# Fused cosine attention and gated product on one core: loads, turns and stores on one queue, V cast on chip, the last pair of each batch turned by TensorE

## The chip, the core and the metric

The kernel runs on one core of a Trainium2 chip. The core has five engines with queues of their own: TensorE (PE, with its weight loads shown as PEld), VectorE (DVE), ScalarE (ACT), GpSimd (POOL) and SyncE (SP). Each runs its instructions in the order in which they were written into its queue, and waits on semaphores for the others. DMA transfers are issued here from SP and from POOL. The metric is the device time of one execution in microseconds.

## The reference

Eight batches, twelve heads, 448 positions of 64 numbers. Rows of q and k are brought to length one, scores are divided by tau = 0.1, softmax and the product with v follow. The result, with heads side by side as 768 columns, goes through two weight products with `h * cos(h)` between them.

```python
q_n = q / (np.linalg.norm(q, axis=-1, keepdims=True) + 1e-06)
k_n = k / (np.linalg.norm(k, axis=-1, keepdims=True) + 1e-06)
scores = np.matmul(q_n, k_n.transpose(0, 1, 3, 2)) / tau
attn = np.exp(scores - np.max(scores, axis=-1, keepdims=True))
attn = attn / (np.sum(attn, axis=-1, keepdims=True) + 1e-09)
x = np.matmul(attn, v).transpose(0, 2, 1, 3).reshape(B * S, H * D)
h = x @ w_in                      # 768 to 2048
return (h * np.cos(h)) @ w_out    # 2048 to 768
```

## The kernel before

**Tiles.** A *pair* is two heads; three pairs are a *unit* (half a batch), six pairs a batch; there are 48 pairs and 16 units. The 448 positions lie as 4 x 112, so most tiles have 112 partitions.

**Work of a unit.** `load` brings k and q as fp32 into `raw` (two buffers, so unit u+2 can be loaded only when unit u has been scaled). `square` makes `sq` (mostly on POOL, line 683), `reduce` sums it on DVE (line 690), `rnorm` makes 1/length on ACT by a logarithm and an exponential (lines 698 and 701), `scale` writes the normed rows to `qks` in bf16 (POOL, line 709). `load_v` brings V through POOL's queue into `vin`, cast to bf16 by the DMA, and `copy_v` copies it to `va`, beside a column of ones (DVE for units 0 to 3, POOL later, line 659).

**Work of a pair.** `transposes` turns `qks` into `qkT`: the first nine pairs by PE and a DVE copy (lines 732, 740), the others by a DMA transpose on SP (line 724). `scores` multiplies on PE into the PSUM tiles SC0 and SC1 (line 749) and ACT takes the exponential into `PX` (line 754). `attend` multiplies with `va` into the PSUM tile AV (line 771), DVE divides by the sums into `xs` (lines 780, 781), and `xs` is turned into `xT`: by a DMA transpose on SP (line 787), except for pairs 4 and 5, which PE turns into the PSUM bank PO (line 795) with a DVE copy behind it (line 799).

**Work of a batch.** `m1` is the first weight product: eight groups of twelve products into SC0, SC1 or AV (line 812), a cosine on ACT (line 826, the sine table with a quarter turn), a product on DVE into `gT` (line 828). It reads all six `xT` of its batch and stands behind the first pair of the next batch. ACT loads another table before and after it (line 606). The second product (M2, line 862) runs by tiles of 128 rows in two halves, 16 products each, into PO or PO2; DVE copies each half to one of three buffers `osb` (line 869), and SP stores the tile (line 873). M2 fills PE's gaps between scores.

**Order.** All operations are written down as a list with reads and writes. `arrange` then plays the list through a table of costs and picks for every engine the next operation that is ready and due first; an operation with a large negative `bias` counts as due early. `emit` writes the queues, computes the waits, and puts idle products on zeros (`zt`, line 897) into long planned gaps of PE. So a changed cost, bias or dependency can move work on all engines. The parts that matter most here:

```python
XPE = (4, 5)
o = P.op(eng, ..., cost=(0.75 if eng == "POOL" else 0.46) * len(fns),
         dma=sem, bulk=bulk, label=label, bias=-100.0 if eng == "POOL" else 0.0)
if p == 0 and 2 <= u < NU - 1:
    load(4, 0, UP, eng="POOL") if u == 2 else None
    copy_v(u + 1)
    load_v(u + 2) if u < NU - 2 else None
if 3 <= u < NU - 2:
    load(u + 2, p, p + 1)
```

Units 2, 3 and 4 and all of V go through POOL's queue, as do the weights W1 and W2 in four parts each (lines 886 and 892); units 0, 1 and those from 5 on go through SP, pair by pair.

Of the kernel before, what the change touches and what calls it, by code (L numbers as in the profile page):

```python
# [482 lines left out]
def bass_cosine_attention__then__act_gcu_kernel(  # L483
# [10 lines left out]
    DM = NH * D  # L494
# [57 lines left out]
    zt = sb("zt", [128, S], BF16)  # L552
    iot = sb("iot", [NP, NP], I32)
# [30 lines left out]
    MM = S / 2400.0 + 0.0025  # L584
    MH = HW / 2400.0 + 0.0025

    def dma(eng, fns, reads, writes, sem, bulk=0.0, label="", behind=None, pkt=0.013):
        o = P.op(eng, lambda e: [f(e) for f in fns], reads, writes, cost=(0.75 if eng == "POOL" else 0.46) * len(fns),
                 dma=sem, bulk=bulk, label=label, bias=-100.0 if eng == "POOL" else 0.0)
        o.nd, o.pkt = len(fns), pkt  # L590
        if behind is not None:
            P.order_only(behind, o)
        return o
# [54 lines left out]
            if eng == "POOL":  # L648
                pooled[0] = P.ops[-1]

    def load_v(u):
        i = u % 2
        dma("POOL", [lambda e: e.dma_start(vin[i].ap().rearrange("p (h c) -> p h c", h=UH), src(v, u, 0, UH))],
            (), [("vin", i)], "vin%d" % i, 2.3, "load v u%d" % u, pooled[0], 0.055)
        pooled[0] = P.ops[-1]

    def copy_v(u):
        i = u % 2
        f = lambda e: e.tensor_copy(vav[i][:, :, 0:D], vinv[i])  # L659
# [103 lines left out]
    def attend(g):  # L763
        u, p, j, y = g // UP, g % UP, g % 2, g % NX
        i, b, n = u % 2, g // PB, D + 1

        def av(e, a):
            for x in range(NJ):
                k = a * S + NP * x
                for c in range(NJ):  # L770
                    t = e.matmul(AVv[:, a, n * x : n * x + n], PXv[j][:, c, k : k + 128],  # L771
                                 vav[i][:, NJ * (2 * p + a) + c, 0:n], start=(c == 0), stop=(c == NJ - 1))
            return t

        P.group = len(P.ops)
        for a in range(2):
            P.op("PE", lambda e, a=a: av(e, a), [("va", i)] + [("PX", j, c) for c in range(NJ)], ["AV"],
                 cost=NJ * NJ * 0.0304, mode="F", label="AV%d" % g)
        P.group = None
        dve(lambda e: e.reciprocal(rcpv[y], AXv[:, :, :, D]), ["AV"], [("rcp", y)], 8 * NS, label="rcp%d" % g)  # L780
        dve(lambda e: e.tensor_tensor(  # L781
            xsv[y].rearrange("p x h d -> p h x d"), AXv[:, :, :, 0:D],
            bass.AP(rcp[y], 0, [[NS, NP], [NJ, 2], [1, NJ], [0, D]]), ALU.mult),
            ["AV", ("rcp", y)], [("xs", y)], NS * D, label="xs%d" % g)
        to = ("xT", b % 2, g % PB)
        if g not in XPE:
            dma("SP", [lambda e: e.dma_start_transpose(
                xTv[b % 2][:, g % PB, :].rearrange("p (x m) -> p x m", x=NJ), xs[y].ap())],
                [("xs", y)], [to], "xT%d" % y, 0.4, "X%d" % g, None, 0.014)
            P.ops[-1].cost = 0.8  # L790
            return

        def turn(e):
            for x in range(NJ):
                r = e.transpose(XTv[:, NP * x : NP * x + NP], xsv[y][:, x, :, :], ident.ap())
# [56 lines left out]
    def m2_emit(n=10 ** 6):  # L852
        for t, hf in m2_queue[:n]:
# [14 lines left out]
            o = t % 3  # L868
            dve(lambda e, po=po, o=o, hf=hf: e.tensor_copy(osb[o].ap()[:, HW * hf : HW * hf + HW], po[:, 0:HW]),  # L869
                keys, [("osb", o, hf)], HW, label="osb%d" % t)  # L870
            if hf == 1:
# [12 lines left out]
    def load_w1(x):  # L884
        w = FF // NQ
        pooled[0] = dma("POOL", [lambda e: e.dma_start(
            W1v[:, :, w * x : w * x + w], bass.AP(moe_w_in.tensor, w * x, [[FF, 128], [128 * FF, NKC], [1, w]]))],
            (), [("W1", x)], "W1_%d" % x, 4.2, "W1.%d" % x, pooled[0], 0.09)

    def load_w2(x):  # L890
        w = NF // NQ
        pooled[0] = dma("POOL", [lambda e: e.dma_start(
            W2v[:, w * x : w * x + w, :], moe_w_out[128 * w * x : 128 * w * (x + 1), :].rearrange("(f p) n -> p f n", p=128))],
            (), [("W2", x)], "W2_%d" % x, 4.2, "W2.%d" % x, pooled[0], 0.13)

    zero = dve(lambda e: e.memset(zt.ap(), 0.0), (), ["zt"], S)  # L896
    P.filler = {n: (lambda e, t=t: e.matmul(t.ap()[:, 0:S], zt.ap()[:, 0:128], zt.ap(), start=True, stop=True))  # L897
                for n, t in (("PO", PO), (("TP", 0), PO2))}, zero, MM, 0.3
# [3 lines left out]
    pairs = [P.ops[-PB + x] for x in range(PB)]  # L902

    def find(label):
        return [o for o in P.ops if o.label == label][-1]
# [43 lines left out]
    norms(0, 0)  # L949
    transposes(0)  # L950
    norms(0, 1)
    load_v(0)
    after(P.ops[-1], pairs[1])
    load_w1(0)
    after(P.ops[-1], pairs[3])
    load_v(1)
    load_w1(1)
    copy_v(0)
    copy_v(1)
    for g in range(PB):  # L960
        pair(g)
    load(2, 0, UP, eng="POOL")
    load_w1(2)
    load_w1(3)
    load_v(2)
    load_w2(0)
    load_w2(1)
    norms(2, 0)
    load(3, 0, UP, eng="POOL")
    load_w2(2)  # L970
    load_w2(3)
    load_v(3)
    for g in range(PB, BYPE):
        transposes(g)
    attend(PB - 1)
# [17 lines left out]
    banks[0] = banks[0] + [(n, x[:, 0, :]) for n, x in PHs]  # L993
    m2_emit()
    P.arrange()
    P.emit(nc, ["out%d" % o for o in range(3)])
    ctx.close()
    return P

# [32 lines left out]
```

## Time and profile before

| | us |
|---|---|
| median of 3 runs | 481.06 |
| lowest and highest run | 480.97, 484.44 |
| the profiled execution, its time | 482.17 |
| its span, first to last instruction | 480.4 |
| PE busy | 444.1 |
| of that, idle products on zeros | 29.2 |
| ACT, DVE, POOL busy | 264.0, 212.8, 209.3 |

The profile shows one execution. A row of a timeline gives the start and the length in us, the engine, the line in the kernel, the operation, the tile written and the tile read, the shapes, how many instructions were merged, and in brackets how long the engine sat idle before and what released it. "SPq" is SP's queue at work on issuing a transfer; the transfer itself lands later. PE is busy for 92% of the span, so what matters is where the other 36 us and the idle products lie, and what stands at the end of those waits. The name of a releaser is that of the instruction which came last; where that instruction had itself been waiting, the cause is one step further back.

### The profile page before, as it was taken

Reading aid. Unit: us, or ns where it says so; the run is one execution under the profiler, and the core shown is the slowest. Engines: PE = TensorE matmul, PEld = TensorE weight load, DVE = VectorE, ACT = ScalarE, POOL = GpSimd, SP = SyncE. Lnnn points to the kernel's source line nnn. Section 1 sums busy time; section 2 is a strip of 40 time slices with the busy share of each in tenths; the row PEclk is TensorE's granted clock in tenths of the full one; section 3 lists DMA queues with packets and bytes.
Section 4 is the critical chain, followed back from the end, with each engine's and each line's share of the span. In section 5 each row is a group of like instructions: output and inputs, shape, how many; then the busy total and the mean of one; then the engine's idle time right before and its main releaser. Section 6 shows DMA issues by size and latency. Waiting matters only on the chain.

```text
span 480.4 us, 8869 instructions
## 1 busy us (share of the span) xinstructions
PE 444.1 (92%) x3787; PEld 236.5 (49%) x3787; DVE 212.8 (44%) x286; ACT 264.0 (55%) x319; POOL 209.3 (44%) x140
## 2 busy tenths in 40 slices
PE   8997999998999499996999949999799999999996
PEld 4453545544555255553555515555445545555563
DVE  5555575537534344353533534435643344225311
ACT  4855368883588125881477604786258756844100
POOL 3988528978088410894029540296408300000000
PEclk9998899999999889997999979999999999999999
DMA  8999998999089910899009990199504700320122
GB/s 220 183 193 202 226 229 102 237 223 246 0 98 216 215 33 0 170 203 222 2 11 163 170 217 0 44 205 210 137 0 107 125 11 1 78 71 0 34 81 84
DMA packets 98919, 59.63 MB, mean 124 GB/s; under 512 B 60896, under 2 KB 94240, under 8 KB 98880
## 3 DMA queue, kind: packets, MB, share of 16 engines
q1 hardware_dynamic: 81472, 43.14, 42.6%
q0 software_dynamic: 17408, 15.93, 22.4%
q8 instruction: 30, 0.49, 0.4%
q14 instruction: 9, 0.07, 0.1%
HBM read 45.61 MB, written 11.01 MB: 118 GB/s over the span
## 4 chain that ended last, share of the span: by engine, by line
PE 56%; POOL 20%; ACT 9%; issue 6%; DMA 5%; DVE 2%; SPq 1%; POOLq 0%; ACTq 0%
PE SC L812 20%; PE AV L812 12%; PE PO L862 11%; POOL qks L709 9%; POOL sq L683 6%; ACT PX L754 5%; PE AV L771 4%; DMA xT<-xs 4%; PE PO L897 3%; PE SC L749 3%; POOL va L659 3%; PE SC L862 2%; ACT L606 2%; DMA raw<-in_q_dram 2%; ACT cosb L826 1%
## 5 line engine op out<-in xcount | busy, mean ns | idle before, releaser
L754 ACT ACTIVATE PX<-SC 112x896 bf16<-112x896 f32 x192 | 164.8, 914 | 30.9 <-PE SC L749 30.8
L862 PE MATMUL PO<-W,gT 128*128 128x384 bf16 x816 | 151.2, 330 | 13.6 <-DVE osb L869 13.6
L709 POOL TENSOR_TENSOR qks<-raw,rn 112x1024 bf16<-112x1024 f32 x47 | 88.6, 1909 | 119.5 <-ACT rn L701 119.4
L812 PE MATMUL SC<-xT,W 128*128 128x448 bf16 x480 | 101.1, 367 | 11.7 <-DMA xT<-xs 9.0
L862 PEld LDWEIGHTS PO<-W,gT 128*128 128x128 bf16 x816 | 73.6, 98 | 74.3 <-issue 19.2
L826 ACT ACTIVATE cosb<-SC,cst 128x896 f32<-128x896 f32 x40 | 40.2, 1007 | 105.0 <-PE SC L812 104.9
L683 POOL TENSOR_TENSOR sq<-raw 112x1024 bf16<-112x1024 f32 x42 | 79.2, 1907 | 34.6 <-DMA raw<-in_q_dram 34.4
L690 DVE TENSOR_REDUCE n<-sq 112x16 f32<-112x1024 bf16 (+1 forms) x49 | 58.3, 1193 | 53.5 <-POOL sq L683 49.0
L812 PEld LDWEIGHTS SC<-xT,W 128*128 128x128 bf16 x480 | 48.0, 101 | 59.8 <-issue 21.0
L828 DVE TENSOR_TENSOR gT<-SC,cosb 128x896 bf16<-128x896 f32 x40 | 43.6, 1091 | 45.7 <-ACT cosb L826 45.4
L749 PE MATMUL SC<-qkT 64*128 64x448 bf16 x384 | 58.2, 357 | 3.7 <-ACT PX L754 0.9
L812 PE MATMUL AV<-xT,W 128*128 128x448 bf16 x288 | 58.5, 352 | 0.7
L771 PE MATMUL AV<-va,PX 112*128 112x65 bf16 x1536 | 57.1, 193 | 0.5 <-ACT PX L754 0.5
L771 PEld LDWEIGHTS AV<-va,PX 112*128 112x128 bf16 x1536 | 51.5, 97 | 10.9 <-issue 8.9
L869 DVE COPY osb<-PO 128x384 f32<-128x384 f32 x51 | 28.2, 553 | 40.8 <-PE PO L862 40.8
L780 DVE RECIPROCAL rcp<-AV 112x8 f32<-112x8 f32 x48 | 9.9, 206 | 74.0 <-PE AV L771 74.0
L812 PEld LDWEIGHTS AV<-xT,W 128*128 128x128 bf16 x288 | 27.7, 98 | 28.6 <-issue 3.1
L826 ACT ACTIVATE cosb<-AV,cst 128x896 f32<-128x896 f32 x24 | 24.2, 1007 | 30.9 <-PE AV L812 30.8
L828 DVE TENSOR_TENSOR gT<-AV,cosb 128x896 bf16<-128x896 f32 x24 | 26.2, 1091 | 25.7 <-ACT cosb L826 25.5
L749 PEld LDWEIGHTS SC<-qkT 64*128 64x128 bf16 x384 | 14.6, 93 | 42.7 <-ACT PX L754 25.9
L781 DVE TENSOR_TENSOR xs<-AV,rcp 112x512 bf16<-112x512 f32 x48 | 33.2, 691 | 2.0
L897 PE MATMUL PO<-zt 128*128 128x448 bf16 x123 | 29.2, 379 | 1.6 <-DVE zt L896 1.6
(37 smaller groups left out, 144.4 us busy)
## 6 DMA issues: line engine op xcount, KB each, us to landing
raw<-in_k_dram SPq DMA_DIRECT2D x39, 224.0 KB, 5.4
raw<-in_q_dram SPq DMA_DIRECT2D x39, 224.0 KB, 6.1
vin<-in_v_dram POOLq DMA_DIRECT2D x16, 336.0 KB, 7.6
W<-in_moe_w_in_dram POOLq DMA_DIRECT2D x4, 768.0 KB, 17.8
W<-in_moe_w_out_dram POOLq DMA_DIRECT2D x4, 768.0 KB, 29.1
out_dram<-osb SPq DMA_DIRECT2D x8, 336.0 KB, 3.6
out_dram<-osb SPq DMA_DIRECT2D x8, 288.0 KB, 2.6
raw<-in_k_dram POOLq DMA_DIRECT2D x3, 672.0 KB, 18.9
```

The source lines that it names most:

```text
L683: pool(lambda e, x=x, y=y: e.tensor_tensor(y, x, x, ALU.mult), src_, dst, 0.1 + n * 1.78e-3, label="sq%d.%d" % (u, p))
L690: dve(lambda e, w=w: e.tensor_reduce(out=n2v[i][:, 2 * p : 2 * p + 2, w], in_=sqv[p][:, :, w, :], axis=mybir.AxisListType.X, op=ALU.add), ...
L709: f = lambda e, s0=s0, s1=s1: e.tensor_tensor(qksv[i][:, p, s0:s1, :, :].rearrange("p s h d -> p h s d"), rawv[i][:, h, s0:s1, :], bass.AP ...
L749: t = e.matmul(SCv[z][:, a, 0:S], qkT[k].ap()[r, NP * c : NP * c + 128], qkT[k].ap()[r, S : 2 * S], start=True, stop=True)
L754: act(lambda e: e.activation(PXv[j][:, c, 0 : 2 * S].rearrange("p (a s) -> p a s", a=2), SCv[z][0:NP, :, 0:S], ACT.Exp, scale=1.0 / TAU), ...
L771: t = e.matmul(AVv[:, a, n * x : n * x + n], PXv[j][:, c, k : k + 128], vav[i][:, NJ * (2 * p + a) + c, 0:n], start=(c == 0), stop=(c == N ...
L781: dve(lambda e: e.tensor_tensor(xsv[y].rearrange("p x h d -> p h x d"), AXv[:, :, :, 0:D], bass.AP(rcp[y], 0, [[NS, NP], [NJ, 2], [1, NJ], ...
L812: t = e.matmul(ph[:, a, 0:S], W1v[:, c, 128 * n : 128 * n + 128], xTv[b % 2][:, c, :], start=(c == 0), stop=(c == NKC - 1))
L826: act(lambda e, ph=ph, cz=cz: e.activation(cosv[cz], ph[:, :, 0:S], ACT.Sin, bias=cst.ap()[:, 0:1], scale=1.0), names(gi) + ["cst0"], [("c ...
L828: dve(lambda e, ph=ph, cz=cz, gi=gi: e.tensor_tensor(gTv[:, 2 * gi : 2 * gi + 2, S * (b % 2) : S * (b % 2) + S], ph[:, :, 0:S], cosv[cz], ...
L862: r = e.matmul(po[:, 0:HW], gTv[:, y, col : col + 128], W2v[:, y, HW * hf : HW * hf + HW], start=(y == 0), stop=(y == NF - 1))
L897: P.filler = {n: (lambda e, t=t: e.matmul(t.ap()[:, 0:S], zt.ap()[:, 0:128], zt.ap(), start=True, stop=True)) for n, t in (("PO", PO), ((" ...
```

## The change

It has six parts, and new costs that go with them.

1. Pairs that PE turns: all of batch 0 and the last pair of every batch (11, 17 ... 47) instead of pairs 4 and 5 only. The turn now goes into AV instead of PO.
2. All loads of q, k and V are issued from SP. Units from 2 on are loaded whole (two transfers of 672 KB instead of six of 224 KB).
3. V stays fp32 in `vin`. `copy_v` casts it, on DVE for units 0 and 1 and on POOL from unit 2 on.
4. V of units 0 and 1 stands between the first loads on SP; the weights wait for V of unit 0, and all but the first two parts of W1 have a small bias (-10) instead of -100, so that unit 2 comes ahead of them in the plan.
5. Four buffers for stores instead of three.
6. The planner's costs of DMA issues, turns, AV products and the V copy are changed.

```diff
-    XPE = (4, 5)
+    XPE = set(range(PB)) | set(range(PB - 1, NG, PB))
+    NO = 4
+    WB = -10.0
-    vin = sbs("vin", 2, [NP, UH * NJ * D], BF16)
+    vin = sbs("vin", 2, [NP, UH * NJ * D], F32)
-    osb = sbs("osb", 3, [128, DM], F32)
+    osb = sbs("osb", NO, [128, DM], F32)
-    XTv = PO.ap().bitcast(BF16)
+    XTv = AV.ap().bitcast(BF16)
...
-        o = P.op(eng, ..., cost=(0.75 if eng == "POOL" else 0.46) * len(fns),
-                 dma=sem, bulk=bulk, label=label, bias=-100.0 if eng == "POOL" else 0.0)
+        o = P.op(eng, ..., cost=(0.8 if eng == "POOL" else 0.52) * len(fns),
+                 dma=sem, bulk=bulk, label=label, bias=bias)
...
-    def load_v(u):
+    def load_v(u, eng="SP"):
...
-        if u < 4:
-            dve(f, [("vin", i)], [("va", i)], UH * NJ * D / 2, lock=True, label="va%d" % u)
+        if u < 2:
+            dve(f, [("vin", i)], [("va", i)], UH * NJ * D, label="va%d" % u)
         else:
-            pool(f, [("vin", i)], [("va", i)], 0.1 + UH * NJ * D * 1.2e-3, label="va%d" % u)
+            pool(f, [("vin", i)], [("va", i)], 1.46, label="va%d" % u)
...
-                [("xs", y)], [to], "xT%d" % y, 0.4, "X%d" % g, None, 0.014)
-            P.ops[-1].cost = 0.8
+                [("xs", y)], [to], "xT%d" % y, 0.7, "X%d" % g, None, 0.014)
+            P.ops[-1].cost = 1.25
...
-        P.op("PE", turn, [("xs", y), "ident"], ["PO"], cost=NJ * 0.0487, mode="F", label="XP%d" % g)
-        dve(lambda e: e.tensor_copy(xTv[b % 2][:, g % PB, :], XTv[:, 0:S]), ["PO"], [to], S, label="xT%d" % g)
+        P.op("PE", turn, [("xs", y), "ident"], ["AV"], cost=NJ * 0.0487, mode="F", label="XP%d" % g)
+        dve(lambda e: e.tensor_copy(xTv[b % 2][:, g % PB, :], XTv[:, 0:S]), ["AV"], [to], S / 2, label="xT%d" % g)
...
     for g in range(PB):
-        load(g // UP, g % UP, g % UP + 1, g == 0, "SP", P.ops[-1] if g else None)
+        load(g // UP, g % UP, g % UP + 1, g == 0)
+        if g % UP == UP - 1:
+            load_v(g // UP)
...
-            load(4, 0, UP, eng="POOL") if u == 2 else None
             copy_v(u + 1)
-            load_v(u + 2) if u < NU - 2 else None
-        if 3 <= u < NU - 2:
-            load(u + 2, p, p + 1)
+            if u == 2:
+                load(4, 0, UP)
+                load_v(4)
+        if 3 <= u < NU - 2 and p == 1:
+            load(u + 2, 0, UP)
+            load_v(u + 2)
...
-    load_v(0)
-    after(P.ops[-1], pairs[1])
     load_w1(0)
-    after(P.ops[-1], pairs[3])
-    load_v(1)
+    after(P.ops[-1], find("load v u0"))
     load_w1(1)
...
-    load(2, 0, UP, eng="POOL")
+    load(2, 0, UP)
```

How the plan moved is seen at three places. The first is SP's queue before batch 3's first product: `xT1<-xs4` and `xT1<-xs5` are the turns of that batch's fifth and sixth pair, `qkT` are turns of later pairs, `raw1` are loads two units ahead. Before:

```order
L787 DMA_TRANSPOSE xT1<-xs4 128x4x112
L724 DMA_TRANSPOSE qkT4<-qks1 128x8x112
L724 DMA_TRANSPOSE qkT5<-qks1 128x8x112
L640 DMA raw1<-in_k_dram 112x2x256
L640 DMA raw1<-in_q_dram 112x2x256
L640 DMA raw1<-in_k_dram 112x2x256
L640 DMA raw1<-in_q_dram 112x2x256
L787 DMA_TRANSPOSE xT1<-xs5 128x4x112
```

After:

```order
L727 DMA_TRANSPOSE qkT4<-qks1 128x8x112
L642 DMA raw1<-in_k_dram 112x6x256
L642 DMA raw1<-in_q_dram 112x6x256
L790 DMA_TRANSPOSE xT1<-xs4 128x4x112
L727 DMA_TRANSPOSE qkT5<-qks1 128x8x112
L876 DMA out_0_dram<-osb2 16x768
L876 DMA out_0_dram<-osb2 112x768
L655 DMA vin1<-in_v_dram 112x6x256
```

The sixth pair's turn is gone from the queue; the fifth pair's now stands behind a whole unit's k and q, and a load of V has come in.

The second is POOL's queue at the start, from the second scale of unit 0 (`qks0`) to the first squares of unit 1 (`sq<-raw1`). Before:

```order
L709 TENSOR_TENSOR qks0<-raw0,rn0 112x2x8x64
L640 DMA raw0<-in_k_dram 112x6x256
L640 DMA raw0<-in_q_dram 112x6x256
L886 DMA W1<-in_moe_w_in_dram 128x6x512 x2
L653 DMA vin0<-in_v_dram 112x6x256
L892 DMA W2<-in_moe_w_out_dram 128x4x768 x2
L683 TENSOR_TENSOR sq0<-raw1 112x1024
```

After:

```order
L889 DMA W1<-in_moe_w_in_dram 128x6x512 x2
L712 TENSOR_TENSOR qks0<-raw0,rn0 112x2x8x64
L686 TENSOR_TENSOR sq0<-raw1 112x1024
L889 DMA W1<-in_moe_w_in_dram 128x6x512 x2
L686 TENSOR_TENSOR sq1<-raw1 112x1024
```

The loads of unit 2 and of V have left POOL, and the other weights have moved behind unit 1's first squares.

The third is DVE's queue ahead of batch 2's first product: `n20` and `n21` are the sums of squares of the next two units, `osb` the copies out of PO and PO2, `gT` the first products of M1. Before:

```order
L869 COPY osb2<-PO 128x384
L690 TENSOR_REDUCE n20<-sq2 112x16
L690 TENSOR_REDUCE n21<-sq0 112x16
L869 COPY osb2<-PO2 128x384
L690 TENSOR_REDUCE n21<-sq2 112x16
L869 COPY osb0<-PO 128x384
L690 TENSOR_REDUCE n21<-sq1 112x16
L828 TENSOR_TENSOR gT<-SC0,cosb0 128x2x448
```

After:

```order
L693 TENSOR_REDUCE n20<-sq0 112x16
L872 COPY osb1<-PO 128x384
L693 TENSOR_REDUCE n20<-sq1 112x16
L693 TENSOR_REDUCE n20<-sq2 112x16
L831 TENSOR_TENSOR gT<-SC0,cosb0 128x2x448
L831 TENSOR_TENSOR gT<-SC1,cosb1 128x2x448
L693 TENSOR_REDUCE n21<-sq0 112x16
L831 TENSOR_TENSOR gT<-AV,cosb0 128x2x448
```

The second unit's sums (`n21`) no longer stand between copies out of PO; they have moved behind M1's first two products.

More of the change, by code (lines that the diff above doesn't have):

```diff
@@ L585, in bass_cosine_attention__then__act_gcu_kernel, with dma @@
     MH = HW / 2400.0 + 0.0025
-    def dma(eng, fns, reads, writes, sem, bulk=0.0, label="", behind=None, pkt=0.013):
-        o = P.op(eng, lambda e: [f(e) for f in fns], reads, writes, cost=(0.75 if eng == "POOL" else 0.46) * len(fns),
-                 dma=sem, bulk=bulk, label=label, bias=-100.0 if eng == "POOL" else 0.0)
+    def dma(eng, fns, reads, writes, sem, bulk=0.0, label="", behind=None, pkt=0.013, bias=0.0):
+        o = P.op(eng, lambda e: [f(e) for f in fns], reads, writes, cost=(0.8 if eng == "POOL" else 0.52) * len(fns),
+                 dma=sem, bulk=bulk, label=label, bias=bias)
         o.nd, o.pkt = len(fns), pkt
@@ L649, in load @@
                 pooled[0] = P.ops[-1]
-    def load_v(u):
+    def load_v(u, eng="SP"):
         i = u % 2
-        dma("POOL", [lambda e: e.dma_start(vin[i].ap().rearrange("p (h c) -> p h c", h=UH), src(v, u, 0, UH))],
-            (), [("vin", i)], "vin%d" % i, 2.3, "load v u%d" % u, pooled[0], 0.055)
-        pooled[0] = P.ops[-1]
+        dma(eng, [lambda e: e.dma_start(vin[i].ap().rearrange("p (h c) -> p h c", h=UH), src(v, u, 0, UH))],
+            (), [("vin", i)], "vin%d%s" % (i, eng), 2.4, "load v u%d" % u, pooled[0] if eng == "POOL" else None, 0.055)
+        if eng == "POOL":
+            pooled[0] = P.ops[-1]
     def copy_v(u):
@@ L777, in attend @@
             P.op("PE", lambda e, a=a: av(e, a), [("va", i)] + [("PX", j, c) for c in range(NJ)], ["AV"],
-                 cost=NJ * NJ * 0.0304, mode="F", label="AV%d" % g)
+                 cost=NJ * NJ * 0.0324, mode="F", label="AV%d" % g)
         P.group = None
@@ L867, in m2_emit @@
                      keys, cost=4 * MH, mode="F", label="M2 %d" % t, stream="B")
-            o = t % 3
+            o = t % NO
             dve(lambda e, po=po, o=o, hf=hf: e.tensor_copy(osb[o].ap()[:, HW * hf : HW * hf + HW], po[:, 0:HW]),
@@ L900, in bass_cosine_attention__then__act_gcu_kernel @@
     for g in range(PB):
-        load(g // UP, g % UP, g % UP + 1, g == 0, "SP", P.ops[-1] if g else None)
-    pairs = [P.ops[-PB + x] for x in range(PB)]
+        load(g // UP, g % UP, g % UP + 1, g == 0)
+        if g % UP == UP - 1:
+            load_v(g // UP)
+    early = [o for o in P.ops if o.eng == "SP" and o.dma is not None]
+    for a, b in zip(early, early[1:]):
+        P.order_only(a, b)
     def find(label):
@@ L961, in bass_cosine_attention__then__act_gcu_kernel @@
         pair(g)
-    load(2, 0, UP, eng="POOL")
+    load(2, 0, UP)
     load_w1(2)
     load_w1(3)
-    load_v(2)
     load_w2(0)
@@ L968, in bass_cosine_attention__then__act_gcu_kernel @@
     norms(2, 0)
-    load(3, 0, UP, eng="POOL")
+    load(3, 0, UP)
+    load_v(2)
+    P.order_only(P.ops[-2], P.ops[-1])
     load_w2(2)
@@ L972, in bass_cosine_attention__then__act_gcu_kernel @@
     load_v(3)
+    P.order_only(find("load v u2"), P.ops[-1])
     for g in range(PB, BYPE):
@@ L995, in bass_cosine_attention__then__act_gcu_kernel @@
     P.arrange()
-    P.emit(nc, ["out%d" % o for o in range(3)])
+    P.emit(nc, ["out%d" % o for o in range(NO)])
     ctx.close()
```

4 lines of the change are left out of this document (2 added, 2 removed).

## The prediction

> **What bounds the kernel now.** I read the page first (busy shares, the 40 slices), then the busy times by batch, then PE's timeline at each gap, and last the queues that ended those gaps. The three page lines say that PE is busy nearly throughout, that its clock falls in a few slices only, and that the DMA engines are full for the first quarter and idle at times later.
>
> ```profile
> PE 444.1 (92%) x3787; PEld 236.5 (49%) x3787; DVE 212.8 (44%) x286; ACT 264.0 (55%) x319; POOL 209.3 (44%) x140
> PEclk9998899999999889997999979999999999999999
> DMA  8999998999089910899009990199504700320122
> ```
>
> The second view cuts the span where each batch's first weight product (M1) starts: batches 1 to 6 in order. Columns: length, busy time of each engine, granted clock, DMA share, GB/s.
>
> ```profile
> 45.17:110.14 64.97, 61.77 (x540) 32.21 (x540) 34.67 (x45) 43.73 (x54) 44.07 (x28) 0.95 1.10 209
> 110.14:170.21 60.07, 53.22 (x457) 28.34 (x458) 30.89 (x39) 31.90 (x38) 35.75 (x21) 0.95 0.81 149
> 170.21:223.63 53.42, 49.29 (x441) 26.22 (x439) 21.14 (x31) 31.90 (x38) 23.25 (x15) 0.98 0.59 114
> 223.63:286.52 62.89, 55.68 (x457) 29.04 (x458) 28.35 (x37) 31.90 (x38) 30.55 (x18) 0.91 0.71 124
> 286.52:339.10 52.58, 49.17 (x441) 26.17 (x439) 21.11 (x30) 31.90 (x38) 23.15 (x15) 1.00 0.64 116
> 339.10:384.77 45.67, 45.28 (x416) 23.91 (x417) 20.25 (x29) 29.95 (x37) 17.79 (x11) 1.00 0.40 84
> ```
>
> The last row is a stretch without a fault: 45.67 us, PE busy for 45.28, clock 1.00. The others are 7 to 19 us longer, a part of it because they hold more W2 products (M2), which must be done somewhere, and a part because PE waits. The waits stand in PE's timeline; brackets give the idle time before the instruction and what ended it.
>
> ```profile
> 45.17 5.76 PE L812 MATMUL SC<-xT,W 128*128 128x448 bf16 x15 [2.39 <-DVE xs L781]
> 104.04 4.15 PE L897 MATMUL PO<-zt 128*128 128x448 bf16 x21
> 110.14 4.70 PE L812 MATMUL SC<-xT,W 128*128 128x448 bf16 x24 [1.96 <-DMA xT<-xs]
> 167.47 2.74 PE L862 MATMUL PO<-W,gT 128*128 128x384 bf16 x8 [6.61 <-DVE osb L869]
> 197.99 1.47 PE L862 MATMUL PO<-W,gT 128*128 128x384 bf16 x8
> 223.63 7.16 PE L812 MATMUL SC<-xT,W 128*128 128x448 bf16 x24 [3.90 <-DMA xT<-xs]
> 283.79 2.74 PE L862 MATMUL PO<-W,gT 128*128 128x384 bf16 x8 [6.98 <-DVE osb L869]
> 339.10 3.19 PE L812 MATMUL SC<-xT,W 128*128 128x448 bf16 x16 [3.18 <-DMA xT<-xs]
> ```
>
> Each batch's M1 starts late, in two ways by turns. A late start also costs a slow clock: eight M2 take 2.74 instead of 1.47 us, 24 M1 take 7.16 instead of 4.70. The windows around two of them show that clock in the column before the DMA share.
>
> ```profile
> 45.17:51.30 6.13, 6.13 (x20) 2.67 (x21) 1.09 (x1) 1.86 (x3) 4.31 (x3) 0.51 1.16 212
> 164.00:167.40 3.40, 0.00 (x0) 0.00 (x0) 1.67 (x2) 0.00 (x0) 3.40 (x2) 0.50 1.10 288
> ```
>
> What ended the waits: first the rows of DVE, of SP's queue and of the chain of waits before the start at 223.63, then those of POOL and DVE before 167.47.
>
> ```profile
> 210.81 0.69 DVE L781 TENSOR_TENSOR xs<-AV,rcp 112x512 bf16<-112x512 f32 x1
> 211.11 3.09 SPq L724 DMA_TRANSPOSE qkT<-qks  x2
> 216.37 1.86 SPq L787 DMA_TRANSPOSE xT<-xs  x1
> 216.37 7.02 DMA xT<-xs
> ...
> 163.80 5.59 POOL L683 TENSOR_TENSOR sq<-raw 112x1024 bf16<-112x1024 f32 x3 [6.85 <-DMA raw<-in_q_dram]
> 165.73 1.22 DVE L690 TENSOR_REDUCE n<-sq 112x16 f32<-112x1024 bf16 x1 [7.52 <-POOL sq L683]
> 166.86 0.55 DVE L869 COPY osb<-PO 128x384 f32<-128x384 f32 x1
> ```
>
> The last pair's xs is ready at 211.5, but SP issues its turn at 216.4, behind two qkT turns and four small loads, and it lands 7.0 later. At 163.8 the squares wait for a late load; DVE, which runs in order, sits 7.5 us at the sum of those squares, and the copy that empties PO stands behind it. The store buffers are not what ends this wait: the copy runs as soon as DVE is free. So a fourth osb alone is worth nothing by this row.
>
> **The change, part by part.**
>
> *Last pair turned by PE.* Price on PE and DVE, and what the DMA path takes (time from issue to landing of xT turns, least, median, most: at the start, then in the stretches 171:224 and 224:287):
>
> ```profile
> 40.49 0.37 PE L795 MATMUL PO<-ident,xs 112*128 112x112 bf16 x4
> DMA to landing us min/median/max: 8.5/12.2/13.2
> DMA to landing us min/median/max: 2.5/5.5/7.0
> DMA to landing us min/median/max: 2.4/6.7/8.0
> ```
>
> Seven later pairs (11, 17 ... 47) add 7 x 0.37 = 2.6 us on PE, which is the bound: all of it counts. The first batch's four more turns fall into stretches that PE now fills with idle products, so 0, unless DVE is late with the copy out of AV, which the next AV product needs; then each costs up to the 1.2 us of a sum standing ahead. Next late is the fifth pair, still turned by DMA. Its AV product is two before the one ahead of M1:
>
> ```profile
> 204.24 1.19 PE L771 MATMUL AV<-va,PX 112*128 112x65 bf16 x32
> 212.75 1.19 PE L771 MATMUL AV<-va,PX 112*128 112x65 bf16 x32
> ```
>
> The sixth pair's product began midway, at 208.5, and its xs ended at 211.5, 3.0 later. The fifth pair's would end at 207.2; with 7.0 to 8.0 to land that is 214.2 to 215.2 if SP is free. M1 could start at about 215.0, after the scores. If SP is held for 0 to 3 us by the loads ahead, the wait is 0 to 3; I take 1.0 for each of five starts, 5.0 in all, since 0 needs a free queue and the small loads have become long ones.
>
> *Loads and V on SP, by whole units.* Per unit SP issues three loads instead of six, and none goes through POOL; 22 POOL issues (16 of V, six of raw) go. POOL gets two casts more.
>
> ```profile
> L659 POOL COPY va<-vin 112x1536 bf16<-112x1536 bf16 x12 | 17.5, 1461 | 6.0 <-PE AV L771 6.0
> L659 DVE COPY va<-vin 112x1536 bf16<-112x1536 bf16 x4 | 6.7, 1670 | 0.6 <-DMA vin<-in_v_dram 0.6
> ```
>
> The cast from fp32 has no row. Below it lies the same copy, 1.46 on POOL; above it a two-input product, 1.9 per 1024 elements (the 5.59 for three squares), which would be 2.8. I take 1.46, since it has one input. Fourteen casts cost 20 us to 39 us of POOL, which is busy for 18 to 36 us of 46 to 60 in these stretches: 0 on the path. V as fp32 has no row either:
>
> ```profile
> raw<-in_k_dram SPq DMA_DIRECT2D x39, 224.0 KB, 5.4
> vin<-in_v_dram POOLq DMA_DIRECT2D x16, 336.0 KB, 7.6
> ```
>
> 672 KB will land in between 5.4 us (as one raw load) and 16.2 (as three, one after the other). I take today's 7.6, and 0 on the path: V is needed a whole unit, over 20 us, later, and the engines are 29 to 60% free from 170 us on. The queue's price is that a V load waits for the cast that frees its buffer, and every turn behind it on SP waits too.
>
> *DVE order and waits.* The sums of the later unit now stand behind the copies out of PO and mostly between M1's products, so a late load no longer stops an M2 tile. I take back: idle 6.61 + 3.90 + 6.98 + 3.18 = 20.7; slow clock 2 x (2.74 - 1.47) + (7.16 - 4.70) = 5.0; at batch 1 the idle products and the wait after them, 4.15 + 1.96 = 6.1. Together 31.8.
>
> *The start.*
>
> ```profile
> 22.25 4.14 POOL L683 TENSOR_TENSOR sq<-raw 112x1024 bf16<-112x1024 f32 x2
> 25.01 3.57 PE L897 MATMUL PO<-zt 128*128 128x448 bf16 x18
> 46.30 0.34 ACT L698 ACTIVATE lnn<-n,cst 112x48 f32<-112x48 f32 x1 [4.77 <-DVE n L690]
> ```
>
> POOL's first square of unit 1 comes at 22.25, straight after seven DMA issues; now it follows a scale, with one pair of W1 issues before that, so PE should lose up to 3.57 us of idle products. But ACT takes the logarithm of unit 2 before M1's first sine, and that unit now shares the engines with the weights, so I count nothing for this. What goes is the 2.39 us wait of M1 for a turn (8.5 to 13.2 us under way here; now none) and the slow clock of its first 15: 5.76 - 15/24 x 4.70 = 2.8. Together 5.2, bounds 0 (unit 2 later by as much) and 8.8 (with the 3.57).
>
> DVE casts V of units 0 and 1 (1.67 each) beside POOL's work. In the trace such a copy beside two squares made these take 4.14, where three took 5.59, 0.4 more than two thirds: that is the price on a chain with slack, 0 in the sum. The Trainium skill (SBUF — State Buffer, "Who interferes with whom") speaks against the edit: a DVE copy or cast that uses both ports locks GpSimd out for its whole length. By that, an estimate, two casts would add 3.3 us to POOL's start and the forecast would be 455; the 0.4 of the row is nearer to none.
>
> **Sum.** -31.8 - 5.2 + 5.0 + 2.6 = -29.4 us. The profiled execution has a span of 480.4 and a time of 482.17, 1.1 above the median of 481.06. So span 451.0, its own time 452.8, median about 452.
>
> **Rivals.**
>
> (a) *Loads as late as before.* The engines carry about the same bytes, so the squares and sums are late anyway and DVE stops PO twice: 6.61 + 6.98 + 2.5 = 16 stay, 468. For: DMA share 0.81 and 0.71 in just these two stretches. Against: the copies now stand ahead of the second unit's sums. The Trainium skill (DMA: Bandwidth & Descriptors, "Issuing engines are not separate DMA queues") says that all queues use the same 16 engines and a move saves only issue time; by that rule alone this rival holds.
>
> (b) *Start starved.* Unit 2 and V go through SP while W1 fills POOL's queue; unit 2's logarithm slips past 46.3 by 5 us and M1 stops: the 5.2 is lost and 5 more, 462.
>
> (c) *Slower: one SP queue in order.* A fifth-pair turn stands behind a whole unit's load or a V load that waits for its cast, and lands as late as at the start, 13.2 instead of 8. Then each of six starts waits 5.2 more, plus 2.5 of slow clock: 46 us, so 498. It decides against the change from 29.4 / 6 = 4.9 us per batch on. For: SP's order puts raw1 right ahead of xs4. Against: 8.0 was the longest once W2 was in.
>
> (d) *Nothing moves:* another engine ends each start at the same time, 476 to 486. Against: PE at 45.28 of 45.67 in the undisturbed stretch, no other engine over 30.
>
> **Chances.** Forecast 0.55 (443 to 460: low end with no residual waits, -5, and the 3.6 at the start; high end with (a) half true), (a) 0.17, (b) 0.13, (c) 0.08, (d) 0.07. The range 443 to 469 takes in the first three. Faster by over 1% (below 476; about what a measurement tells from no change) holds for the first three, 0.85; the same 0.07; slower 0.08.
>
> **What would show it.** Right: no osb or xT wait of over 2 us on PE after 110 us, clock 1.00 in every batch after the first, stretches of 45 to 50 us, fewer idle products before 30 us. Wrong: a DVE sum that idles over 5 us with an osb copy behind it (a); ACT's logarithm of unit 2 after 50 us (b); xT of the fifth pair landing over 10 us after its xs (c).

## The result, and the profile after

The changed kernel takes 463.96 us (median of four runs, 461.91 to 465.73), and the kernel before 481.82 in runs beside it (480.97 to 484.44). The ratio is 0.962, with a 95% interval of 0.956 to 0.968: 3.8% faster. It lies inside the whole range of 443 to 469, but above the forecast's own 443 to 460, and 12 us over the 452 named. The profiled execution took 465.73 us, its span is 463.9; all rows of after below are of that one.

The page of the changed kernel first: busy shares, clock and DMA by slices, then the rows of M2, of M1 in both of its tiles and of the scores. The last part of a row is the idle time in front and what ended it.

```profile
PE 435.5 (94%) x3800; PEld 235.8 (51%) x3800; DVE 216.5 (47%) x295; ACT 263.5 (57%) x319; POOL 195.0 (42%) x120
PEclk9799999999999999999999999989999999999999
...
L865 PE MATMUL PO<-W,gT 128*128 128x384 bf16 x816 | 148.8, 326 | 0.0
L815 PE MATMUL SC<-xT,W 128*128 128x448 bf16 x480 | 97.2, 357 | 8.8 <-DMA xT<-xs 6.9
L752 PE MATMUL SC<-qkT 64*128 64x448 bf16 x384 | 58.2, 358 | 7.1 <-DVE qkT L743 4.6
L815 PE MATMUL AV<-xT,W 128*128 128x448 bf16 x288 | 58.5, 352 | 5.2 <-DVE gT L831 4.8
```

M2 waits for nothing now (13.6 us for osb before), and the clock falls in two slices. M1 still waits for xT, and two waits have come up: M1 for `gT`, the scores for `qkT`.

The second view is the table by batch again, cut where each M1 starts (length; busy time of PE, weight loads, DVE, ACT, POOL; clock; DMA share; GB/s).

```profile
0.00:44.96 44.96, 36.31 (x377) 20.11 (x377) 29.05 (x37) 26.62 (x40) 29.34 (x28) 0.92 1.09 228
44.96:104.24 59.28, 57.72 (x541) 31.31 (x538) 33.44 (x46) 41.77 (x53) 39.37 (x22) 1.00 0.93 213
104.24:154.58 50.34, 45.54 (x421) 24.03 (x421) 24.98 (x34) 33.48 (x40) 29.49 (x17) 1.00 0.79 166
154.58:207.45 52.87, 49.43 (x445) 26.38 (x446) 26.03 (x35) 32.23 (x39) 27.27 (x16) 1.00 0.71 158
207.45:254.84 47.39, 45.37 (x420) 24.10 (x421) 22.75 (x31) 31.55 (x38) 24.23 (x14) 1.00 0.57 132
254.84:303.39 48.55, 45.54 (x421) 24.03 (x421) 22.96 (x32) 32.22 (x39) 24.51 (x15) 1.00 0.69 144
303.39:352.67 49.28, 49.01 (x433) 25.91 (x434) 22.73 (x32) 29.97 (x37) 20.80 (x12) 0.97 0.52 115
```

The first start of M1 comes no earlier (44.96, 45.17 before). The six others come 5.9 to 35.7 us earlier, the last of them 32.1, but the end of the span only 16.5: M2 products have moved behind the last start, where 752 products of PE now fill 111.23 us, against 656 in 95.63 before. So the stretches between the starts don't compare one by one, and all behind the second M1 is taken together here. Set beside the forecast, with its terms put where their rows lie (one of the five residual waits and one of the seven turns in the second line):

| part of the span | before, us | after, us | gain | forecast gain |
|---|---|---|---|---|
| up to the first M1 | 45.17 | 44.96 | 0.2 | 2.4 |
| first M1 to second M1 | 64.97 | 59.28 | 5.7 | 2.8 + 6.1 - 1.0 - 0.4 = 7.5 |
| second M1 to the end | 370.26 | 359.66 | 10.6 | 20.7 + 5.0 - 4.0 - 2.2 = 19.5 |
| sum | 480.4 | 463.9 | 16.5 | 29.4 |

Most of what is missing lies behind the second M1. PE's timeline shows it: the waits in M1 of batches 1 to 5.

```profile
112.73 4.70 PE L815 MATMUL SC<-xT,W 128*128 128x448 bf16 x24 [1.51 <-DVE gT L831]
123.36 2.43 PE L815 MATMUL AV<-xT,W 128*128 128x448 bf16 x12 [1.39 <-DVE gT L831]
154.58 4.70 PE L815 MATMUL SC<-xT,W 128*128 128x448 bf16 x24 [1.77 <-DMA xT<-xs]
167.72 2.43 PE L815 MATMUL AV<-xT,W 128*128 128x448 bf16 x12 [1.63 <-DVE gT L831]
172.96 2.43 PE L815 MATMUL AV<-xT,W 128*128 128x448 bf16 x12 [0.55 <-DVE gT L831]
207.45 4.70 PE L815 MATMUL SC<-xT,W 128*128 128x448 bf16 x24 [1.13 <-DMA xT<-xs]
254.84 4.70 PE L815 MATMUL SC<-xT,W 128*128 128x448 bf16 x24 [1.79 <-DMA xT<-xs]
271.73 2.43 PE L815 MATMUL AV<-xT,W 128*128 128x448 bf16 x12 [0.55 <-DVE gT L831]
303.39 6.38 PE L815 MATMUL SC<-xT,W 128*128 128x448 bf16 x24 [2.20 <-DMA xT<-xs]
```

The four waits for xT add up to 6.9 us, and the last is followed by slow clock (24 products in 6.38 instead of 4.70). The five for `gT` add up to 5.6. Their source is in the timelines of POOL and DVE ahead of 167.72:

```profile
163.43 5.59 POOL L686 TENSOR_TENSOR sq<-raw 112x1024 bf16<-112x1024 f32 x3 [7.48 <-DMA raw<-in_q_dram]
...
165.35 1.22 DVE L693 TENSOR_REDUCE n<-sq 112x16 f32<-112x1024 bf16 x1 [3.90 <-POOL sq L686]
166.49 1.08 DVE L831 TENSOR_TENSOR gT<-AV,cosb 128x896 bf16<-128x896 f32 x1
```

It is the chain of before with another last link: a late load, the squares, a sum at which DVE stands, and behind that sum the product that empties AV instead of the copy that empties PO.

At the start, PE waits 4.00 us for `qkT` at 20.39. DVE's timeline, POOL's and PE's:

```profile
12.71 0.62 DVE L743 COPY qkT<-PO 128x896 bf16<-128x896 bf16 x1 [0.59 <-PE PO L735]
13.25 6.46 DVE L662 CAST va<-vin 112x1536 bf16<-112x1536 f32 x1
19.64 0.61 DVE L743 COPY qkT<-PO 128x896 bf16<-128x896 bf16 x1
...
12.94 1.85 POOL L889 DMA_DIRECT2D W<-in_moe_w_in_dram  x2
14.80 1.92 POOL L712 TENSOR_TENSOR qks<-raw,rn 112x1024 bf16<-112x1024 f32 x1
16.66 1.90 POOL L686 TENSOR_TENSOR sq<-raw 112x1024 bf16<-112x1024 f32 x1
18.50 2.45 POOL L889 DMA_DIRECT2D W<-in_moe_w_in_dram  x2
...
20.39 0.56 PE L752 MATMUL SC<-qkT 64*128 64x448 bf16 x2 [4.00 <-DVE qkT L743]
```

The cast of V stands on DVE for 6.46 us, while POOL issues W1, scales and squares without a gap, and the copy that PE needs stands behind it.

### The profile page after: what moved, and what is told of

It reads as the page before. It is cut to its first block, busy times and chain, and to the rows that moved or that the text cites. A ratio compares the mean times of both kernels' runs of the same rounds, so it can differ in the third digit from the quotient of the medians.

```text
span 463.9 us, 8849 instructions
## 1 busy us (share of the span) xinstructions
PE 435.5 (94%) x3800; PEld 235.8 (51%) x3800; DVE 216.5 (47%) x295; ACT 263.5 (57%) x319; POOL 195.0 (42%) x120
## 4 chain that ended last, share of the span: by engine, by line
PE 57%; DMA 14%; ACT 10%; DVE 7%; POOL 5%; issue 3%; SPq 3%; ACTq 0%
PE PO L865 20%; DMA raw<-in_q_dram 11%; PE SC L815 10%; PE AV L815 8%; PE AV L774 8%; PE SC L752 6%; ACT PX L757 6%; POOL qks L712 3%; DMA xT<-xs 3%; PE PO L900 2%; PE SC L865 2%; DVE gT L831 2%; DVE va L662 2%; SPq L727 2%; DVE n L693 2%
## 5 line engine op out<-in xcount | busy, mean ns | idle before, releaser
L865 PE MATMUL PO<-W,gT 128*128 128x384 bf16 x816 | 148.8, 326 | 0.0
L815 PE MATMUL SC<-xT,W 128*128 128x448 bf16 x480 | 97.2, 357 | 8.8 <-DMA xT<-xs 6.9
L815 PEld LDWEIGHTS SC<-xT,W 128*128 128x128 bf16 x480 | 46.4, 99 | 55.1 <-issue 14.4
L774 PEld LDWEIGHTS AV<-va,PX 112*128 112x128 bf16 x1536 | 52.5, 98 | 12.6 <-issue 10.8
L662 POOL CAST va<-vin 112x1536 bf16<-112x1536 f32 x14 | 20.5, 1462 | 18.5 <-PE AV L774 17.9
```

Source lines behind the costliest of these rows:

```text
L815: t = e.matmul(ph[:, a, 0:S], W1v[:, c, 128 * n : 128 * n + 128], xTv[b % 2][:, c, :], start=(c == 0), stop=(c == NKC - 1))
L865: r = e.matmul(po[:, 0:HW], gTv[:, y, col : col + 128], W2v[:, y, HW * hf : HW * hf + HW], start=(y == 0), stop=(y == NF - 1))
```

## The experiments

Four theories came out of these rows. One: late loads now hold the products of M1, by way of the sums in front of them. Two: the fifth pair's turn ends the start of M1. Three: the cast on DVE loses the start. Four: the prediction's own, that the turns by PE carry the xT part of the gain and the new loads little. All kernels are compared with the kernel before in runs on the same chip. "Re-planned" means that the planner orders the whole program anew; the others keep the order of every engine.

**The V casts as a two-input operation** (order kept):

```
-        f = lambda e: e.tensor_copy(vav[i][:, :, 0:D], vinv[i])
+        f = lambda e: (e.tensor_tensor(vav[i][:, :, 0:D], vinv[i], vinv[i], ALU.max) if u < 2 else ...)
```

> The changed kernel with one thing altered: DVE turns V of units 0 and 1 into bf16 as the maximum of V with itself, a form with two fp32 inputs, in the same place; the order on every engine is the same. Theory (the one-input fp32 cast is held up by POOL, 6.46 us for the first, and the start loses by it what the other edits gain there): the first V instruction takes under 2.2 us, the qkT copy behind it runs by 16 instead of at 19.64 us, PE's 4.00 us wait at 20.39 goes and the clock stays full between 17 and 24 us; M1 of the first batch starts 3 to 5.5 us earlier than 44.96, and the time is 458.5 to 461 us, against 464.0. Rival 1 (the loads set the start: the DMA share is 1.09 up to 45 us): the instruction gets short, but M1 starts at 44 to 45 and the time is 463 to 465. Rival 2 (not POOL but the load of V or something else holds the instruction): it still takes over 4 us.

466.33 us, ratio 0.968 (0.962 to 0.973). The instruction takes longer:

```profile
13.21 7.11 DVE L662 TENSOR_TENSOR va<-vin 112x1536 bf16<-112x1536 f32 x1
```

So the number of inputs is not what matters, and the theory as put falls. The load is not the cause either: V of unit 0, issued at 3.7, landed 8.2 us later, at 11.9, in both traces.

**The products of the fifth and sixth pair last** (re-planned):

```
-            m1(points[g])
+            m1(points[g], 2, PB - 2)
```

> The changed kernel, but in M1 of batches 1 to 6 the first two groups run their products of the first four pairs before those of the fifth and sixth, so that M1 needs the fifth pair's xT only after 16 products (about 3 us). The planner makes the whole order anew. Theory (the fifth pair's turn by DMA ends the waits at the starts of M1: 1.77 + 1.13 + 1.79 + 2.20 us, and 1.7 us of slow clock at the last of them): no wait of M1 for xT over 0.5 us, time 8.6 us less at most and 5 at least, 455.5 to 459. Rival (M1 is held by its cosine products on DVE anyway, so that an earlier start is lost again a few us later): waits for gT grow by what the waits for xT lose, time 461.5 to 464.

465.16 us, ratio 0.964 (0.960 to 0.969): no gain, as the rival said. The waits have changed places:

```profile
165.88 4.11 PE L815 MATMUL AV<-xT,W 128*128 128x448 bf16 x12 [3.16 <-DVE gT L831]
206.94 1.69 PE L815 MATMUL SC<-xT,W 128*128 128x448 bf16 x8 [1.13 <-DMA xT<-xs]
267.56 3.76 PE L815 MATMUL AV<-xT,W 128*128 128x448 bf16 x12 [4.36 <-DVE gT L831]
```

Waits for xT fall from 6.9 to 1.1 us, and those for `gT` go from 1.63 and 0.55 to 3.16 and 4.36 at batches 2 and 4, with slow clock behind (12 products in 4.11 instead of 2.43).

**The later unit's sums behind M1's products** (re-planned):

```
+    for n, o in enumerate(last):                 # o: M1's last product of batch n + 1
+        for p in range(UP):
+            if 2 * n + 7 < NU:
+                P.order_only(o, find("red%d.%d" % (2 * n + 7, p)))
```

> The changed kernel with an order forced on DVE: the three sums of the later unit stand behind M1's last product with the cosine in each of batches 1 to 5, and in batch 1 the first sum stands behind the second such product. The planner makes the rest of the order anew. Theory (a sum that waits for a late load holds the products behind it, and PE then waits for the tile: 1.51 + 1.39 us at batch 1, 1.63 + 0.55 at batch 2, 0.55 at batch 4): PE waits for gT under 0.3 us in M1 of these batches, each M1 lasts at most 19.3 us instead of up to 22, time 4 to 6 us less: 458 to 460. Rival (the sums come later, so the logarithm, the scaling and the turns of that unit come later and hold the scores or a load): the gT waits go, but waits for qkT or raw take their place and the time is 463 to 466.

461.74 us, ratio 0.957 (0.954 to 0.961). In M1 of batches 1 to 5 one wait for `gT` over 0.5 us is left (0.66, in batch 1), but those for xT rise from 6.9 to 10.2 us, the longest two being

```profile
251.24 6.38 PE L815 MATMUL SC<-xT,W 128*128 128x448 bf16 x24 [2.37 <-DMA xT<-xs]
303.25 6.38 PE L815 MATMUL SC<-xT,W 128*128 128x448 bf16 x24 [4.27 <-DMA xT<-xs]
```

The time is about 2 us under the 463.5 to 464.0 of the changed kernel, short of the 4 to 6 expected, and the two intervals overlap.

**Three output buffers** (order kept): each copy out of PO waits for the store three tiles back.

> The changed kernel in the same order on every engine, but each copy out of PO waits for the store three tiles back, as with three output buffers (one of the four still serves, only the wait is that of three). Theory (the fourth buffer is worth nothing): 464 within 1.5 us, no wait for a store over 0.5 us ahead of a copy. Rival (the wait for the M2 tiles before the change was one for a store buffer after all): PE waits for osb again, several us in all, 467 or more.

467.20 us, ratio 0.967 (0.962 to 0.972); the profiled execution took 463.85. The view of the tile osb names all that its 56 copies waited for:

```profile
  PE PO L865: 60.5, 31
  PE SC L865: 8.2, 4
  PE AV L865: 2.1, 1
```

That is M2 itself, never a store. The other three runs, at 466.9 to 467.7, lie above all of the changed kernel's (466.3 at most, in two sets), so the times don't exclude a cost of some 3 us; the trace shows no place for one.

**The changed kernel again**, beside the next three.

> The changed kernel once more, to have its time on the same chip as the next three. Both theories: ratio to before 0.957 to 0.968 as in its first run; waits for xT and gT on PE within M1 of some 11 us together. The first V cast starts close to POOL's first issue of W1: if it starts first it takes under 2 us, if later over 6 us.

463.49 us, ratio 0.960 (0.955 to 0.966). The waits for xT and `gT` come to some 13 us, where 11 were expected. The cast of the same kernel now takes

```profile
13.05 1.13 DVE L662 CAST va<-vin 112x1536 bf16<-112x1536 f32 x1
24.77 4.37 DVE L662 CAST va<-vin 112x1536 bf16<-112x1536 f32 x1
```

POOL's first issue of W1 begins at 13.31 here, after the cast, and at 12.94, ahead of it, in the first trace. In eight traces of kernels with fp32 V on SP and a cast or a maximum, the first V instruction took 0.95 to 1.62 us in the five where it began no later than that issue, and 6.33 to 7.11 in the three where it began later. M1 of the first batch starts at 43.59 instead of 44.96, no more, since now the second cast is held: PE waits 2.96 us for the xT copy behind it.

**V as a sum over one element** (order kept):

```
-        f = lambda e: e.tensor_copy(vav[i][:, :, 0:D], vinv[i])
+        f = lambda e: (e.tensor_reduce(out=vav[i][:, :, 0:D], in_=vinv[i].unsqueeze(3), axis=..., op=ALU.add) if u < 2 else ...)
```

> The changed kernel with V of units 0 and 1 turned into bf16 on DVE as a sum over one element (one input, not the copy's form), in the same place and order. The maximum of two inputs was held up as the cast was (7.11 us). Theory (what holds it is the pair of ports that DVE shares with POOL, which a copy, a cast and a product of two inputs in SBUF all need, and a sum does not): both take 1.6 to 1.9 us whenever they start, as the sums n beside POOL's products do (1.2 for 1024 elements); no wait for qkT at 20 us or for xT at 30 us over 1 us; M1 of the first batch starts at 40.5 to 43 instead of 43.8 to 47.1; time 1.5 to 4 us under that of the changed kernel in these runs. Rival (any DVE instruction from SBUF stands still while POOL runs): over 3 us each and no gain.

463.97 us, ratio 0.961 (0.955 to 0.966). The mechanism is as the theory says, with POOL's issue ahead of it once more:

```profile
12.66 1.84 POOL L889 DMA_DIRECT2D W<-in_moe_w_in_dram  x2
...
13.23 1.74 DVE L662 TENSOR_REDUCE va<-vin 112x1536 bf16<-112x1536 f32 x1
23.98 1.74 DVE L662 TENSOR_REDUCE va<-vin 112x1536 bf16<-112x1536 f32 x1
```

M1 of the first batch starts at 39.05, 4.5 us earlier than in the last trace, but the time is the same, so the gain expected didn't come. The tables by batch of the changed kernel (its second trace) and of this one say where it goes:

```profile
102.40:153.45 51.05, 45.53 (x421) 24.03 (x421) 23.67 (x32) 33.76 (x40) 28.02 (x16) 1.00 0.79 163
```

```profile
98.94:153.13 54.19, 47.16 (x422) 24.43 (x421) 23.71 (x32) 33.88 (x40) 28.06 (x16) 0.97 0.77 156
```

The second M1 still starts 3.5 us earlier, the third 0.3: batch 1 gives it back in waits for `gT` (1.85 and 2.13 us, the second with slow clock; 1.67 and 1.68 in the changed kernel) and for xT (2.97 against 2.04, both with slow clock).

**Both orders together** (re-planned): the edits of the second and third experiment.

> The changed kernel with both orders of before together: the later unit's sums behind M1's products, and the fifth and sixth pair's products last in the first two groups of M1. Theory (at the start of M1 two waits stand one behind the other, xT and then gT, and each alone covers the other, which is why the second edit alone gave nothing and the first left 10.2 us of xT waits): together they take away both, waits for xT and gT in M1 of batches 1 to 6 under 3 us together, time 455 to 458 against 464, 4 to 7 us under the sums alone by the profile's sums of waits. Rival (a third wait follows: M1 starts earlier, and the qkT turns, the loads or the scores behind it are late by as much): 460 to 462, as with the sums alone.

454.11 us, ratio 0.941 (0.936 to 0.946): 9.4 us under the changed kernel on the same chip (463.49), and more than the sum of what either edit gave. The table by batch from the second M1 on:

```profile
100.09:145.67 45.58, 45.32 (x422) 24.07 (x422) 22.89 (x31) 32.06 (x39) 25.27 (x14) 1.00 0.83 177
145.67:192.88 47.21, 45.47 (x421) 23.98 (x421) 24.39 (x33) 32.05 (x39) 28.94 (x16) 1.00 0.70 160
192.88:240.90 48.02, 46.13 (x425) 24.36 (x425) 23.24 (x33) 32.06 (x39) 21.60 (x13) 1.00 0.65 140
```

PE is busy for 45.32 of 45.58 us, where it was busy for 45.54 of 50.34. All waits of M1 for xT and `gT` over 0.5 us, after the first batch, come to 5.4 (1.48, 1.62, 2.34). Unlike what was expected, that is more than 3, and the time is still lower than 455: in this trace the first M1 starts at 39.76, which the edits weren't meant to do. The re-planned order splits POOL's second pair of W1 issues, and the two casts take 0.95 and 2.51 us.

**All three** (re-planned):

> The last one with V of units 0 and 1 as a sum over one element as well. Theory: the gains add, 452 to 456. Rival (the start is bound by the loads, so that an earlier first M1 waits later for raw or W): as sums and fifth, within 1 us.

452.86 us, ratio 0.939 (0.933 to 0.945): the fastest, but no different from the last within the intervals. It can't tell the rival from the theory, since the first M1 starts at 39.90 here and at 39.76 there.

**The turns alone**, in the kernel before (re-planned): its `XPE`, and AV for the turn, are those of the change.

> The kernel before with only the first part of the change: x of each batch's last pair and of all six pairs of the first batch turned by PE, through AV. Loads, V and stores are as before; the planner makes the order anew. Theory (the prediction's sum: turns take away the waits of M1 for the sixth pair, 1.96 + 3.90 + 3.18 + 2.39 us, the idle products before the first of them and the slow clock behind them, some 17 us, for 2.6 of turns and 5.0 of the fifth pair's wait; the waits for osb, 13.6 us and 2.5 of slow clock, are a matter of the loads and the order on DVE and stay): 471 to 477. Rival 1 (the new order that comes with any edit also moves the sums away from the copies, so that the osb waits go too): 458 to 468. Rival 2 (turns alone are worth nothing, as the loads hold the squares, sums and scores by as much): 479 to 484.

The four times are 465.4, 476.0, 480.1 and 481.3 us, beside 478.8 to 489.8 of the kernel before: too far apart for a ratio. The profile is of the run of 476.0, 10.6 us above the lowest, so its waits need not be those of every run. It shows no wait of M2 for osb, but these of M1:

```profile
155.05 7.60 PE L812 MATMUL SC<-xT,W 128*128 128x448 bf16 x24 [5.86 <-DMA xT<-xs]
...
217.82 6.94 PE L812 MATMUL SC<-xT,W 128*128 128x448 bf16 x24 [6.24 <-DVE gT L828]
```

So the order that comes with the turns takes away the waits for osb without the new loads, against the theory; stalls of 6 us stand in front of M1's products. How much the turns alone are worth stays open.

**Without the last pairs' turns**, in the changed kernel (re-planned):

```
-    XPE = set(range(PB)) | set(range(PB - 1, NG, PB))
+    XPE = set(range(PB))
```

> The changed kernel without the turns by PE of the last pair of batches 1 to 7 (pair 11, 17 ... 47 go by DMA again; the first batch's six stay). Theory: M1 of these batches waits for the sixth pair's DMA, 3 to 6 us at each of six or seven starts with slow clock behind, less 2.6 us for turns and less the fifth pair's 7 to 9: 470 to 485, and no wait for osb over 1 us. Rival (the turns are worth nothing): 460 to 466.

475.22 us (472.26 to 478.58), ratio 0.987 (0.974 to 1.000), against 0.960 of the changed kernel. M1 waits for xT 10.3 us in all:

```profile
160.84 7.53 PE L815 MATMUL SC<-xT,W 128*128 128x448 bf16 x24 [3.83 <-DMA xT<-xs]
217.34 4.70 PE L815 MATMUL SC<-xT,W 128*128 128x448 bf16 x24 [1.81 <-DMA xT<-xs]
273.08 6.04 PE L815 MATMUL SC<-xT,W 128*128 128x448 bf16 x24 [3.08 <-DMA xT<-xs]
```

By the medians (475.2 against 463.5 to 464.0) the seven turns, with the order that comes with them, carry some 12 us of the gain of 18 to 21. Idle products come back too (123 instead of 92). M2 waits for no osb here either, so that part of the gain doesn't hang on the turns.

**V by POOL's cast DMA** (re-planned): `vin` is bf16 again and `load_v` issues on POOL; one order rule between the loads of unit 3 and V of unit 2 goes with it, and all else is as changed.

> The changed kernel with V loaded as before: cast to bf16 by the DMA, issued by POOL; the other loads, the turns and the stores are as changed. Theory (V's way is worth little by itself, since V is needed a whole unit later): 460 to 467, the fp32 casts' hold at the start gone but POOL's issues of V back. Rival (V out of POOL's queue is what lets the squares run in time): POOL's squares begin later, waits for osb or gT of over 8 us in all come back, 470 to 478.

467.42 us, ratio 0.971 (0.960 to 0.981): as the theory said in kind, though 0.4 us above its range. M1 waits 5.2 us for xT and 1.7 for `gT`. By the medians V's way is worth some 3.5 us, which the intervals don't separate from none. The Trainium skill (DMA: Bandwidth & Descriptors, "Issuing engines are not separate DMA queues") says that transfers started by any engine run on the same 16 DMA engines, and that starting them from several engines saves only the time of issuing; this run agrees so far as it can tell.

## Why the prediction came out as it did

**The direction and most of the mechanism were right.** Waits of M2 for osb were put at 13.59 us and are 0.0. The turns cost what was counted (13 of them, 4.8 us on PE, 0.37 each). The cast on POOL, bounded by 1.46 and 2.8, takes 1.46. V in fp32 lands in 8.2 us, where 7.6 was taken. The fourth osb is worth nothing that the trace shows. Of rival (b), the logarithm of unit 2 does slip, to 48.80 from 46.30, but not past 50.

**That the time lies between 443 and 469 is in part luck.** The range went past 460 for rivals (a) and (b), at 468 and 462, and neither came as it was put: no tile of M2 waits for osb, and the logarithm slips by 2.5 us instead of 5. Of the prediction's signs of being right, three were missed: a wait for xT of 2.20 us, a clock of 0.97 in the stretch behind it, and stretches of 50.34 and 52.87 us behind the second M1 (45 to 50 was the sign). A sign of being wrong, that of rival (c), came as well (see below).

**"So a late load no longer stops an M2 tile" was right, and the sum from it wrong.** The 20.7 us were taken back whole. The sums had moved behind M1's first products, which the order printed ahead of the prediction shows, and those products empty the three tiles on which M1 runs. So the hazard of rival (a) stayed and moved: 5.6 us of waits for `gT`, priced at nothing. It should have been asked of the moved sum who stands behind it in its new place, as of the old one.

**"I take 1.0 for each of five starts" was too low.** Four starts wait 1.77, 1.13, 1.79 and 2.20 us, and the last has 1.7 of slow clock behind it: 8.6, against 5.0 (4.0 of it behind the second M1). With the 5.6 this is 10.2 us that the sum left out, where 8.9 are missing behind the second M1. Behind these waits stands the mechanism of rival (c), at a smaller price. Its sign was an xT of the fifth pair that lands over 10 us after its xs, and at the four starts that wait it landed 11.1, 14.3, 11.1 and 11.5 us after. At the last of them xs was ready at 291.66:

```profile
292.39 6.40 SPq L727 DMA_TRANSPOSE qkT<-qks  x2
298.84 1.27 SPq L790 DMA_TRANSPOSE xT<-xs  x1
298.84 4.31 DMA xT<-xs
```

The transfer itself took 3.0 to 7.5 us; 6.5 to 8.1 went by before SP issued it, mostly in the two qkT turns ahead. Such a pair of turns took 5.4 to 6.4 us here, shortly behind a whole unit's loads, and 2.6 to 3.8 elsewhere in this trace; that the loads are the cause was not tested. M1 waited only 1.1 to 2.2 us for it, not the 5.2 of rival (c), because PE had other work until 9.5 us after that xs (13.4 at batch 3), where the prediction counted 7.8 (207.2 to 215.0).

**The two are not added but stand one behind the other.** Each edit alone (465.16 and 461.74) moved the wait to the other place, and both together gave 9.4 us. That is shown by the three runs and by the waits in their traces, with one reserve: the re-planned order also started the first M1 3.8 us earlier. As the same early start gave nothing by itself in the kernel with V as a sum, the edits to M1 are needed for it to count.

**"Price on a chain with slack, 0 in the sum" failed for the cast on DVE.** The row of before (1.67 for the bf16 copy) was read as the copy's own work; the 6.46, 4.37 and 1.13 us of one and the same cast show that such a row can be mostly wait, and that the length hangs on what POOL has begun. The bf16 copy itself took 0.56 us with V loaded by POOL, where POOL stood idle as it began (at 11.44), and 1.98 beside POOL's issues of weights and V (at 15.69). The Trainium skill (SBUF — State Buffer, "Who interferes with whom") says that copies and casts in a two-port mode, and DVE instructions with two inputs in SBUF (against POOL's reads), contend with POOL for one pair of ports, while a reduction never does. The traces agree in kind: 6.46 for the cast, 7.11 for the maximum, 1.74 for the sum, each begun after POOL's issue. The prediction's estimate from it, 455, moved towards the measured time, but not for the reason it gave, as the total below shows. By that section the second comer waits for one instruction of the other, but here DVE stood through POOL's issue, its scale and its square (12.94 to 18.56), and the maximum likewise. For the total, though, a freed cast was worth nothing measurable (463.97 against 463.49): an earlier start alone is given back in batch 1, where the waits for `gT` and xT stand.

**What stays open:** the value of the turns alone, and whether V's new way is worth 0 or 3.5 us.

## What to carry to other kernels

When an instruction is moved away from a stall, look at what stands behind it on its engine in the new place, and price the same lateness there. Where two waits lie one behind the other, take away both before judging either edit: each alone gave 2 us or nothing, the two together 9, with a re-planned start beside them. A duration beside another engine's work may be mostly a wait; compare the same instruction at several places before using it as a price.

## What the runs showed of the hardware

- The first fp32 to bf16 cast of 112x1536 on DVE took 0.95 to 1.62 us where it began no later than POOL's first issue of W1, and 6.33 and 6.46 where it began later; the second, begun during a square on POOL in all seven traces with two casts, took 2.42 to 4.37. Written as a sum over one element it took 1.74 both times, beside the same work of POOL.
- POOL pays too when DVE goes first: two issues of W1 took 2.12 us behind such a cast and 1.85 otherwise, and a scale 2.62 instead of 1.90.
- In the thirteen traces together, 20 of the 23 waits of 2.0 us or more ahead of M1's products were followed by slow clock (the others were 2.26, 2.34 and 3.18 us), and none of the shorter ones, up to 1.98 us.
